# Narrower filler products at the start of a gated attention kernel, with a new order of its steps

## The chip, the cores and the metric

The kernel runs on one core of a Trainium2 chip. The metric is device time in microseconds (us); before the change it is 326.56 us, the median of three runs. One execution was also profiled, and all views of the profile in this document come from such an execution.

The core has five queues of instructions that run side by side, each in its own order: TensorE (PE; its weight loads stand apart as PEld), VectorE (DVE), ScalarE (ACT), GpSimd (POOL) and SyncE (SP). Here SP issues nearly all transfers; POOL issues some, and ACT a few at the start and the end.

## The reference

Attention without a softmax, an RMS norm, and a causal gated unit, all in float32. Batch is 8, there are 8 heads of 64, 576 tokens, and a model width of 512.

```python
kv = np.einsum('bhsd,bhse->bhde', k, v)
out = np.einsum('bhsd,bhde->bhse', q, kv)
rms = np.sqrt(np.mean(out * out, axis=-1, keepdims=True) + 1e-06)
x = out / rms * g_norm              # then (B,H,S,D) -> (B,S,H*D)
...
gate_pre[t] = sum over k of conv_w[k] * xp[t + k]   # 5 taps, causal
gate = 1.0 / (1.0 + np.exp(-gate_pre))
val = x @ w_val
return gate * val @ w_out
```

The three weights of the gated unit arrive as 64-bit floats, and the kernel turns them into float32 itself.

## The kernel before

The order of everything is written out by hand. A text, PLAN, lists 1152 steps such as `kv_product 1 0`; a loop at the end calls the function of each name with those numbers, and each function issues its instructions at once. So PLAN sets the order on every queue. What waits for what follows from the data: an instruction waits only where its operands, or a buffer that it overwrites, are not ready.

**The steps of one batch.** load_q_rows (batches 0 and 1) or load_q bring q, load_half brings one half of the heads of k or v. turn_q_rows turns q on TensorE by products with an identity matrix (L469, into five PSUM banks named qTps), and sort_q copies the result into qT on ACT (L476); from batch 2 on turn_q does this on DVE (L455, L458). kv_product is 36 products of 64x64 for one half of the heads (L435), and kv_copy moves the result to kvbd on ACT (L443). raw_product or raw_pair multiply qT by it (L490, L507). Then comes the norm: square on ACT (L525), sums on DVE (L533), powers on POOL (L539), and normalise on ACT, eight instructions of 64 columns (L551), or for batch 0 in one instruction on DVE (L555). turn_x and keep_x (TensorE L566, ACT L573), or turn_blocks and move_blocks (DVE L579, transfers issued by POOL L587), put x with channels on the partitions into xT; halo copies the edges on POOL.

gate_start, four gate_tap and gate_end make the gate on ACT and DVE. val_product (L616), or for batches 2 to 7 val_fast with its sums (L666), multiplies by w_val. gated joins gate and value on DVE; out_product (L697, L704), or fast_product with its sums (L763), multiplies by w_out. store writes rows out from SP's queue (L796), store_last for the last rows also from ACT's.

**Weights.** stage_weight loads a piece of a weight as 64-bit words (L334), and narrow_weight makes float32 of it in eight small steps, three on ACT and five on DVE. `cw` holds the taps and g_norm; turn_cw and keep_cw turn it.

**The opening.** q, k and v of batch 0 and two pieces of w_val are requested first. TensorE's first instructions are start_warm 36: products of an identity matrix whose result nothing reads. After them come turn_q_rows 0 0 to 0 4, kv_product 0 0 and 0 1, one keep_warm (another unread product, 512 columns wide, L426), turn_cw, and the first raw_product. The q of batch 1 is loaded into a buffer that turn_q_rows of batch 0 reads, and on SP's queue that load stands ahead of seven others: the rest of q, k and v of batch 1 and two pieces of w_val.

Of the kernel before, what the change touches and what calls it, by code (L numbers as in the profile page):

```python
# [21 lines left out]
turn_q_rows 0 1; sort_q 0 0; narrow_weight cw 0 0; turn_q_rows 0 2; sort_q 0 1; narrow_weight cw 0 1;  # L22
turn_q_rows 0 3; narrow_weight cw 0 2; sort_q 0 2; turn_q_rows 0 4; narrow_weight cw 0 3; sort_q 0 3;
kv_product 0 0; narrow_weight cw 0 4; load_q_rows 1 0; narrow_weight cw 0 5; sort_q 0 4; load_half k 1 0;
narrow_weight cw 0 6; narrow_weight cw 0 7; load_half v 1 0; load_q_rows 1 1; kv_product 0 1; load_half k 1 1;
stage_weight wval 2; keep_warm 1; turn_cw; stage_weight wval 3; kv_copy 0; load_half v 1 1; raw_product 0 3;
load_half k 2 0; narrow_weight wval 0 0; raw_product 0 2; keep_cw; square 0 3; narrow_weight wval 1 0;
raw_product 0 4; sums 0 3; load_half v 2 1; square 0 2; raw_product 0 1; narrow_weight wval 0 1; powers 0 3;
sums 0 2; raw_product 0 0; load_half v 2 0; square 0 1; square 0 4; narrow_weight wval 0 2; powers 0 2;
normalise 0 3; narrow_weight wval 1 1; sums 0 1; narrow_weight wval 1 2; turn_x 0 3; sums 0 4; keep_x 0 3;  # L30
powers 0 4; normalise 0 2; square 0 0; narrow_weight wval 0 3; sums 0 0; turn_x 0 2; powers 0 1;
narrow_weight wval 1 3; turn_q_rows 1 0; normalise 0 4; narrow_weight wval 0 4; keep_x 0 2; turn_q_rows 1 1;
narrow_weight wval 1 4; sort_q 1 0; narrow_weight wval 0 5; powers 0 0; turn_x 0 4; normalise 0 1; sort_q 1 1;
turn_q_rows 1 2; narrow_weight wval 1 5; keep_x 0 4; narrow_weight wval 0 6; turn_x 0 1; halo 0;
turn_q_rows 1 3; normalise 0 0; keep_x 0 1; narrow_weight wval 0 7; sort_q 1 2; turn_x 0 0;
narrow_weight wval 3 0; sort_q 1 3; kv_product 1 0; keep_x 0 0; gate_start 0 0; turn_q_rows 1 4;
gate_start 0 1; gate_tap 0 0 3; kv_product 1 1; load_q 2 0; narrow_weight wval 3 1; narrow_weight wval 1 6;
narrow_weight wval 3 2; val_product 0 0 1; gate_tap 0 0 2; kv_copy 1; narrow_weight wval 1 7; load_half k 2 1;
sort_q 1 4; stage_weight wout 0; narrow_weight wval 2 0; gate_start 0 2; gate_tap 0 1 3; raw_product 1 3;
narrow_weight wval 3 3; gate_tap 0 2 3; raw_product 1 2; square 1 3; gate_tap 0 1 2; narrow_weight wval 2 1;  # L40
val_product 0 1 1; sums 1 3; square 1 2; gate_tap 0 2 2; narrow_weight wval 2 2; powers 1 3; load_q 2 2;
narrow_weight wval 3 4; keep_val 0 0 1; raw_product 1 1; sums 1 2; keep_val 0 1 1; narrow_weight wval 2 3;
narrow_weight wval 3 5; powers 1 2; turn_q 2 0; raw_product 1 0; load_q 2 1; square 1 1; normalise 1 3;
val_product 0 0 0; sums 1 1; narrow_weight wval 2 4; stage_weight wout 2; powers 1 1; gate_tap 0 0 1;
square 1 0; normalise 1 2; raw_product 1 4; narrow_weight wval 3 6; turn_x 1 3; narrow_weight wval 2 5;
sums 1 0; val_product 0 1 0; square 1 4; narrow_weight wval 2 6; load_q 2 3; keep_x 1 3; powers 1 0;
gate_tap 0 1 1; normalise 1 1; narrow_weight wval 3 7; turn_x 1 2; kv_product 2 0; narrow_weight wout 0 0;
keep_x 1 2; sums 1 4; stage_weight wout 3; narrow_weight wval 2 7; narrow_weight wout 0 1; powers 1 4;
turn_x 1 1; gate_tap 0 0 0; narrow_weight wout 0 2; kv_product 2 1; gate_tap 0 2 1; narrow_weight wout 0 3;
turn_q 2 1; normalise 1 0; val_product 0 2 1; narrow_weight wout 0 4; load_q 3 0; turn_q 2 2; keep_x 1 1;  # L50
narrow_weight wout 2 0; keep_val 0 1 0; val_product 0 2 0; normalise 1 4; narrow_weight wout 0 5;
narrow_weight wout 0 6; keep_val 0 0 0; val_sums 0; kv_copy 2; stage_weight wout 1; gate_tap 0 1 0; turn_x 1 0;
load_q 3 1; narrow_weight wout 2 1; val_product 0 3 1; turn_q 2 3; keep_x 1 0; gate_end 0 0;
narrow_weight wout 2 2; gated 0 0; turn_x 1 4; narrow_weight wout 2 3; raw_pair 2 3; narrow_weight wout 0 7;
load_half k 3 0; keep_x 1 4; keep_val 0 2 0; narrow_weight wout 3 0; gate_tap 0 2 0; val_product 1 0 1;
square 2 3; load_q 3 2; square 2 2; sums 2 3; keep_val 0 2 1; gate_end 0 1; sums 2 2; powers 2 3;
val_product 1 0 0; gate_end 0 2; narrow_weight wout 2 4; gate_start 0 3; load_half v 3 0;
narrow_weight wout 2 5; gated 0 1; narrow_weight wout 3 1; powers 2 2; narrow_weight wout 2 6;
val_product 1 1 1; normalise 2 3; turn_q 3 0; narrow_weight wout 2 7; load_q 3 3; keep_val 1 0 0; halo 1;
turn_q 3 1; val_product 0 3 0; normalise 2 2; gate_tap 0 3 3; load_half v 3 1; narrow_weight wout 1 0;  # L60
keep_val 0 3 1; gate_tap 0 3 2; load_half k 3 1; raw_pair 2 1; keep_val 1 1 1; keep_val 1 0 1; turn_blocks 2 3;
narrow_weight wout 1 1; raw_product 2 4; turn_blocks 2 2; square 2 1; val_product 1 1 0;
narrow_weight wout 1 2; sums 2 1; square 2 0; gated 0 2; powers 2 1; keep_val 0 3 0; narrow_weight wout 3 2;
gate_tap 0 3 1; val_product 1 2 1; narrow_weight wout 1 3; load_q 4 0; sums 2 0; square 2 4;
narrow_weight wout 3 3; powers 2 0; sums 2 4; gate_tap 0 3 0; normalise 2 1; val_product 1 2 0;
narrow_weight wout 3 4; narrow_weight wout 1 4; powers 2 4; normalise 2 0; turn_blocks 2 1; val_product 1 3 1;
narrow_weight wout 1 5; narrow_weight wout 3 5; turn_q 3 2; normalise 2 4; narrow_weight wout 1 6; load_q 4 1;
kv_product 3 0; gate_end 0 3; narrow_weight wout 3 6; gate_start 1 0; gated 0 3; turn_x 2 4; val_product 1 3 0;
turn_blocks 2 0; keep_x 2 4; gate_start 1 2; narrow_weight wout 3 7; move_blocks 2 3; keep_val 1 1 0;
narrow_weight wout 1 7; gate_start 1 1; kv_product 3 1; gate_tap 1 0 3; keep_val 1 3 0; gate_tap 1 0 2;  # L70
out_product 0 1; kv_copy 3; load_half k 4 1; gate_tap 1 1 3; keep_val 1 2 0; turn_q 3 3; keep_val 1 2 1;
keep_val 1 3 1; gate_tap 1 0 1; load_q 4 2; gate_tap 1 0 0; move_blocks 2 2; gate_tap 1 2 3; raw_pair 3 3;
gate_tap 1 2 2; out_product 0 3; square 3 3; gate_tap 1 2 1; gate_end 1 0; sums 3 3; square 3 2; keep_out 0 1;
gated 1 0; powers 3 3; sums 3 2; store 0 1; gate_start 1 3; gate_tap 1 1 2; out_product 0 0; keep_out 0 3;
gate_tap 1 2 0; powers 3 2; load_half k 4 0; gate_tap 1 1 1; gate_end 1 2; store 0 3; gate_tap 1 3 3;
normalise 3 3; gate_tap 1 1 0; move_blocks 2 1; gate_tap 1 3 2; out_product 0 2; gate_end 1 1; load_half v 4 1;
gate_tap 1 3 1; keep_out 0 0; normalise 3 2; gate_tap 1 3 0; store 0 0; gated 1 1; gate_end 1 3; gated 1 2;
raw_pair 3 1; load_half v 4 0; gated 1 3; turn_q 4 0; raw_product 3 4; move_blocks 2 0; square 3 1;
out_product 0 4; turn_blocks 3 3; square 3 0; sums 3 1; load_q 4 3; val_sums 1; square 3 4; powers 3 1;
turn_q 4 1; turn_q 4 2; load_q 5 0; out_product 0 5; turn_blocks 3 2; keep_out 0 4; sums 3 0; normalise 3 1;  # L80
sums 3 4; powers 3 0; val_sums 2; turn_blocks 3 1; x_sums 2 2; out_product 0 7; halo 2; normalise 3 0;
val_sums 3; weight_sums 0; x_sums 2 0; gate_start 2 2; powers 3 4; keep_out 0 2; gate_tap 2 2 3;
gate_start 2 1; kv_product 4 0; x_sums 2 1; normalise 3 4; turn_q 4 3; kv_product 4 1; load_half v 5 0;
turn_blocks 3 0; load_q 5 1; gate_tap 2 2 2; turn_x 3 4; kv_copy 4; val_fast 2 0 0; x_sums 2 3; keep_x 3 4;
gate_start 2 0; gate_tap 2 1 3; raw_pair 4 3; store 0 4; move_blocks 3 3; val_keep 2 0 0; gate_tap 2 2 1;
val_fast 2 0 1; square 4 3; square 4 2; load_half v 5 1; sums 4 3; val_fast 2 0 2; gate_tap 2 2 0; powers 4 3;
val_fast 2 0 3; val_keep 2 0 2; sums 4 2; val_keep 2 0 1; keep_out 0 5; weight_sums 1; val_fast 2 0 4;
gate_end 2 2; store 0 5; powers 4 2; val_fast 2 0 5; val_keep 2 0 4; keep_out 0 7; gate_tap 2 0 3;
# [106 lines left out]
def kernel(  # L195
# [11 lines left out]
    nc = tc.nc  # L207
# [631 lines left out]
```

## Time and profile before

| | |
|---|---|
| three runs | 326.56, 325.11, 326.56 us |
| the profiled execution | 325.28 us |
| its span, first to last instruction | 323.5 us |
| mean granted TensorE clock | 0.994 |
| data moved by transfers | 55.50 MB, 172 GB/s on average |
| L697, 128 passes | 57.3 us busy |
| L421, 72 passes | 15.6 us busy |
| L435, the 1008 passes from buffers of k and v | 17.0 us busy |

A row of a group gives busy time, which can overlap itself on TensorE, since matmuls are pipelined. A product in float32 is two passes in the profile, so its count is twice that in the code. "Idle" is time of that engine alone.

### The profile page before, as it was taken

Reading aid. Unit: us, or ns where it says so; the run is one execution under the profiler, and the core shown is the slowest. Engines: PE = TensorE matmul, PEld = TensorE weight load, DVE = VectorE, ACT = ScalarE, POOL = GpSimd, SP = SyncE. Lnnn points to the kernel's source line nnn. Section 1 sums busy time; section 2 is a strip of 40 time slices with the busy share of each in tenths; the row PEclk is TensorE's granted clock in tenths of the full one; section 3 lists DMA queues with packets and bytes.
Section 4 is the critical chain, followed back from the end, with each engine's and each line's share of the span. In section 5 each row is a group of like instructions: output and inputs, shape, how many; then the busy total and the mean of one; then the engine's idle time right before and its main releaser. Section 6 shows DMA issues by size and latency. Waiting matters only on the chain.

```text
span 323.5 us, 8361 instructions
## 1 busy us (share of the span) xinstructions
PE 314.0 (97%) x3195; PEld 228.9 (71%) x3195; DVE 253.0 (78%) x451; ACT 191.7 (59%) x542; POOL 137.0 (42%) x177
## 2 busy tenths in 40 slices
PE   8998899999999999999999999999999999999994
PEld 8996787777754557566766667577758885888583
DVE  1014869999999997899899898999997989576612
ACT  1046689999959465785765868566863453224120
POOL 2003808334359447582866366578909200000000
PEclk9999799999999999999999999999999999999999
DMA  7819959699577929887976997322135303122233
GB/s 278 292 32 371 373 159 316 169 268 289 161 201 195 299 53 263 259 243 209 253 178 204 247 284 218 96 66 66 33 97 134 85 13 74 27 65 65 58 75 97
DMA packets 26696, 55.50 MB, mean 172 GB/s; under 512 B 6166, under 2 KB 8214, under 8 KB 26656
## 3 DMA queue, kind: packets, MB, share of 16 engines
q1 hardware_dynamic: 22608, 46.61, 49.8%
q0 software_dynamic: 3168, 6.32, 8.1%
q10 hardware_dynamic: 880, 2.03, 1.7%
q8 instruction: 25, 0.41, 0.6%
q14 instruction: 15, 0.12, 0.2%
HBM read 39.21 MB, written 9.44 MB: 150 GB/s over the span
## 4 chain that ended last, share of the span: by engine, by line
PE 85%; ACT 8%; DMA 3%; DVE 1%; POOL 1%; issue 1%; POOLq 0%; DVEq 0%; ACTq 0%
PE out L697 17%; PE va L666 14%; PE a L763 8%; PE vc L666 7%; PE cb L763 7%; PE val L616 6%; PE warm L421 5%; PE raw L435 5%; PE raw L507 3%; ACT x L551 3%; PE qTps L469 3%; PE out L704 3%; PE vb L666 3%; PE raw L490 2%; DMA v<-in_v_dram 2%; PE xTps L566 1%
## 5 line engine op out<-in xcount | busy, mean ns | idle before, releaser
L539 POOL TENSOR_TENSOR rt<-ss,mhalf 128x8 f32<-128x8 f32 (+1 forms) x40 | 71.7, 1805 | 85.1 <-DVE ss L533 85.0
L604 DVE SCALAR_TENSOR_TENSOR gate<-xT,cwT,gate 128x576 f32<-128x576 f32 x128 | 100.8, 809 | 5.2 <-ACT gate L598 4.7
L587 POOL DMA_DIRECT2D xT<-y x96 | 53.0, 558 | 28.9 <-ACT gv L675 8.2
L551 ACT ACTIVATE x<-raw,rt 128x64 f32<-128x64 f32 x252 | 55.9, 368 | 2.7 <-POOL rt L539 2.7
L697 PE MATMUL out<-wout,gv 128*128 128x512 f32 x128 | 57.3, 595 | 0.0
L697 PEld LDWEIGHTS out<-wout,gv 128*128 128x128 f32 x128 | 24.0, 190 | 26.1 <-issue 24.3
L616 PE MATMUL val<-xT,wval 128*128 128x288 f32 x128 | 33.0, 410 | 0.2 <-ACT xT L573 0.2
L525 ACT ACTIVATE sq<-raw 128x512 f32<-128x512 f32 (+1 forms) x40 | 21.6, 561 | 14.2 <-PE raw L507 10.1
L533 DVE TENSOR_REDUCE ss<-sq 128x8 f32<-128x520 f32 (+1 forms) x40 | 24.7, 632 | 6.4 <-ACT sq L525 6.2
L611 ACT ACTIVATE gate<-gate 128x576 f32<-128x576 f32 x32 | 22.1, 704 | 10.3 <-DVE gate L604 10.2
L616 PEld LDWEIGHTS val<-xT,wval 128*128 128x128 f32 x128 | 23.5, 190 | 6.5 <-ACT xT L573 0.3
L666 PE MATMUL va<-xs,vsum 128*128 128x288 f32 x96 | 27.2, 406 | 0.0
L629 DVE TENSOR_TENSOR gv<-gv,gate 128x576 f32<-128x576 f32 x32 | 23.6, 750 | 3.2 <-ACT gv L687 1.6
L598 ACT ACTIVATE gate<-xT,cwT 128x576 f32<-128x576 f32 x32 | 25.2, 796 | 0.9 <-DVE gv L629 0.9
L666 PEld LDWEIGHTS va<-xs,vsum 128*128 128x128 f32 x96 | 18.2, 190 | 4.9
L712 ACT COPY ot<-out 128x512 f32<-128x512 f32 x20 | 11.9, 594 | 15.7 <-PE out L704 8.7
L435 PEld LDWEIGHTS raw<-v,k 64*64 64x64 f32 x1008 | 15.6, 135 | 4.3 <-issue 1.7
L772 DVE TENSOR_TENSOR ot<-cb,ot 128x256 f32<-128x256 f32 x16 | 6.7, 420 | 13.9 <-ACT ot L776 7.9
L507 PEld LDWEIGHTS raw<-kvbd,qT 64*64 64x64 f32 x768 | 12.3, 134 | 7.1 <-issue 2.7
L435 PE MATMUL raw<-v,k 64*64 64x64 f32 x1008 | 17.0, 220 | 0.3 <-issue 0.3
L579 DVE STREAM_TRANSPOSE y<-x 128x512 f32<-128x512 f32 x24 | 16.5, 692 | 0.9 <-ACT x L551 0.9
L421 PE MATMUL warm<-ident 128*128 128x32 f32 x72 | 15.6, 401 | 1.4 <-POOL ident masks.py:199 1.4
(112 smaller groups left out, 523.3 us busy)
## 6 DMA issues: line engine op xcount, KB each, us to landing
qs<-in_q_dram SPq DMA_DIRECT2D x96, 140.0 KB, 4.8
out_dram<-ot SPq DMA_DIRECT2D x140, 64.0 KB, 1.8
k<-in_k_dram SPq DMA_DIRECT2D x14, 576.0 KB, 6.3
v<-in_v_dram SPq DMA_DIRECT2D x12, 576.0 KB, 6.7
xT<-y POOLq DMA_DIRECT2D x96, 64.0 KB, 3.6
y<-in_moe_w_val_dram SPq DMA_DIRECT2D x4, 512.0 KB, 11.1
w_wout<-in_moe_w_out_dram SPq DMA_DIRECT2D x4, 512.0 KB, 5.3
qs<-in_q_dram SPq DMA_DIRECT2D x3, 576.0 KB, 5.3
```

The source lines that it names most:

```text
L421: nc.tensor.matmul(warm_bank()[:, 0, 0:TB], ident[:], ident[:, 0:TB], start=True, stop=True)
L435: nc.tensor.matmul(raws[r * D:(r + 1) * D, s, i * D:(i + 1) * D], st["k", b, i][rows, r, cols], st["v", b, i][rows, r, cols], start=(j == ...
L533: nc.vector.reduce_sum(out=ss[:, 0:n], in_=st["sq", b, c][:, 0:n], axis=AX.X)
L539: nc.gpsimd.tensor_tensor(out=rt[:, 0:n], in0=st["ss", b, c][:, 0:n], in1=mhalf[:, 0:n], op=ALU.pow)
L551: nc.scalar.activation(out=x[:, to * D:(to + 1) * D], in_=one, func=AF.Copy, scale=st["rt", b, c][:, h:h + 1])
L587: nc.gpsimd.dma_start(out=xTs[b % 2][i * TB:(i + 1) * TB, :, first:first + P], in_=y[a * TB:(a + 1) * TB, i])
L598: nc.scalar.activation(out=gate[:], in_=xTs[b % 2][:, jt, HALO:SX], func=AF.Copy, scale=cwT[:, K - 1, jt:jt + 1])
L604: nc.vector.scalar_tensor_tensor(out=gate[:], in0=xTs[b % 2][:, jt, tap * TB:tap * TB + S], scalar=cwT[:, tap, jt:jt + 1], in1=gate[:], op ...
L616: nc.tensor.matmul(val[:], wval[:, kc, jt * P:(jt + 1) * P], xTs[b % 2][:, kc, HALO + n * SV:HALO + (n + 1) * SV], start=(kc == 0), stop=( ...
L666: nc.tensor.matmul(st[bank, "val", b, mj][:], weights_[:, k], tokens()[:, k], start=(n in (0, 1, 3) and k == 0), stop=(k == NK // 2 - 1), ...
L697: nc.tensor.matmul(po[:], gv[:, jt, first:first + P], wout[:, jt, :], start=(jt == 0), stop=(jt == NK - 1),)
L763: nc.tensor.matmul(st[bank, i, p], tokens()[:, k], weights_[:, k], start=(n < 2 and k == 0), stop=(k == NK // 2 - 1), skip_group_check=True)
```

## The change

Two things change. The filler product uses the first 32 columns of the identity as weights, where it used all 128, and writes 32 rows of its PSUM bank in place of 128. The count of 36 stays.

```diff
     def start_warm(n):
         for _ in range(n):
-            nc.tensor.matmul(warm_bank()[:, 0, 0:TB], ident[:], ident[:, 0:TB], start=True, stop=True)
+            nc.tensor.matmul(warm_bank()[0:TB, 0, 0:TB], ident[:, 0:TB], ident[:, 0:TB], start=True, stop=True)
```

And PLAN's steps stand in another order. The steps are the same but for one more `keep_warm 1`; most move by 10 to 20 places. The opening, cut to what TensorE and SP do:

```diff
 start_warm 36; turn_q_rows 0 0; turn_q_rows 0 1; sort_q 0 0; ... turn_q_rows 0 4;
-kv_product 0 0; load_q_rows 1 0; load_half k 1 0; load_half v 1 0; load_q_rows 1 1; kv_product 0 1; load_half k 1 1;
-stage_weight wval 2; keep_warm 1; turn_cw; stage_weight wval 3; kv_copy 0; load_half v 1 1; raw_product 0 3;
+kv_product 0 0; load_q_rows 1 0; load_half k 1 0; load_half v 1 0; load_q_rows 1 1; keep_warm 1; kv_product 0 1;
+load_half k 1 1; stage_weight wval 2; keep_warm 1; turn_cw; stage_weight wval 3; kv_copy 0; load_half v 1 1; raw_product 0 3;
 ...
-turn_x 0 3; turn_x 0 2; turn_q_rows 1 0; turn_q_rows 1 1; turn_x 0 4; turn_q_rows 1 2; turn_x 0 1; turn_q_rows 1 3;
-turn_x 0 0; kv_product 1 0; turn_q_rows 1 4; kv_product 1 1; val_product 0 0 1;
+turn_x 0 3; turn_x 0 2; kv_product 1 0; turn_x 0 4; turn_q_rows 1 0; turn_q_rows 1 1; turn_x 0 1; turn_q_rows 1 2;
+turn_x 0 0; turn_q_rows 1 3; turn_q_rows 1 4; kv_product 1 1; val_product 0 0 1;
```

Farther on, the loads of k and v change places too, as do the gates, sums and stores between them. From load_half v 4 1 to the kv_product that reads it there were 52 steps and are now 22; from load_half k 7 1 there were 71 and are now 24; from load_half k 6 1 there were 28 and are now 83.

## The prediction

> **What bounds the kernel now.** I read the page's busy row first, then the chain of work that ended last, then the opening in detail: the transfers' landings, the rows of one tile at a time, the waits of SP's queue, and busy time by stretch.
>
> ```profile
> PE 314.0 (97%) x3195; PEld 228.9 (71%) x3195; DVE 253.0 (78%) x451; ACT 191.7 (59%) x542; POOL 137.0 (42%) x177
> PE 85%; ACT 8%; DMA 3%; DVE 1%; POOL 1%; issue 1%; POOLq 0%; DVEq 0%; ACTq 0%
> ```
>
> TensorE is the bound: busy for 314.0 of 323.5 us and 85% of the chain. So a microsecond of TensorE that does no needed work is a microsecond of the end, as long as what follows can move up. The chain (start us, us, what) shows such work at its head:
>
> ```profile
> 1.36 15.57 PE warm L421 x72
> 16.93 5.31 PE qTps L469 x72
> 22.24 2.26 PE raw L435 x144
> 24.50 1.07 PE warm L426 x2
> 25.61 0.23 PE cwps L405
> 25.85 2.00 PE raw L490 x16
> ...
> 40.99 1.21 PE raw L435 x72
> 42.19 0.59 PE qTps L469 x8
> 42.78 1.21 PE raw L435 x72
> 43.99 2.14 PE val L616 x8
> ```
>
> The fillers, L421, hold TensorE from 1.36 to 16.93; 36 products are 72 passes (an f32 product stands as two), 15.57 / 72 = 216 ns each. Are they waiting room for data? The transfers issued in the first 4 us (last column: us from issue to landing):
>
> ```profile
> v<-in_v_dram ACTq DMA_DIRECT2D x2, 576.0 KB, 9.4
> k<-in_k_dram SPq DMA_DIRECT2D x2, 576.0 KB, 9.2
> y<-in_moe_w_val_dram SPq DMA_DIRECT2D x2, 512.0 KB, 11.8
> qs<-in_q_dram ACTq DMA_DIRECT2D x1, 576.0 KB, 5.5
> qs<-in_q_dram SPq DMA_DIRECT2D x1, 576.0 KB, 5.3
> ```
>
> Both parts of q are issued at 0.74 us, so they are in at 6.0 and 6.25. The two halves of k and v, issued from 1.20 to 1.70, land in pairs at about 9.4 and 12.4. All that turn_q_rows and kv_product need is there long before 16.93; only the fillers ahead of it in TensorE's queue hold it back. They hold the loads back too: SP's queue stands behind the release of the q buffer.
>
> ```profile
> SPq L319 <- PE qTps L469: 16.0, 1, 16.0
> ```
>
> **The clock in the opening.** The granted clock reads 1.00 there, but durations (min/median/max ns) say otherwise. First the fillers' rows, then L469 before and after 19.4 us:
>
> ```profile
> L421 PEld LDWEIGHTS warm<-ident x72: 287/333/333, 1.4 to 16.5; 128*128 128x128 f32 x72
> L421 PE MATMUL warm<-ident x72: 401/401/421, 1.4 to 16.5; 128*128 128x32 f32 x72
> ...
> L469 PEld LDWEIGHTS qTps<-ident,qs x24: 183/230/230, 16.9 to 19.1; 128*64 128x64 f32 x24
> L469 PE MATMUL qTps<-ident,qs x22: 421/421/477, 16.9 to 19.1; 128*64 128x128 f32 x22
> ...
> L469 PE MATMUL qTps<-ident,qs x50: 272/273/354, 19.3 to 22.0; 128*64 128x128 f32 x50
> L469 PEld LDWEIGHTS qTps<-ident,qs x46: 137/137/138, 19.5 to 21.9; 128*64 128x64 f32 x46
> ```
>
> The same product takes 421 ns before 19.4 and 273 after, and all fillers have the slow figures. So 15 us of fillers did not raise the clock; 2.5 us of real products did.
>
> **The change, part by part.**
>
> *1. Fillers.* Weights of 32 columns, 32 rows of output; the count stays 36. A slow load took 333 ns for 128 columns and 230 for 64: 103 ns per 64 columns, so 1.6 ns a column, 51 ns for 32. At 216 ns a pass the old filler is just the load of its 128 columns; the 32 moving columns (53 ns at the slow rate, from L469's pairs of 128 columns every 213 ns) lie under it. A new pass is then the larger of 51 and 53 ns. Here a rule speaks against: the Trainium skill, "TensorE: Matmul & The Clock Gate", Part 3, says that a load overlaps running matmuls only when its row group differs. These all use the same rows, so by the rule a pass is 51 + 53 = 104 ns and the 72 end at 1.36 + 7.5 = 8.9 us. But L490 has 128 columns of weights (a load row of 190 ns) and 128 moving on the same rows, and its 16 passes take 2.00 us, 125 ns each: loads do overlap. I take 60 ns, 72 x 60 = 4.3, end at 5.7 us, with ends at 53 ns (5.2 us) and 104 ns (8.9 us).
>
> *2. turn_q_rows of batch 0* now waits for q: start 6.3 us. Its 36 pairs cost 213 ns slow (7.7 us in all) or 109 fast (3.9). The same page, Part 1, has one busy window of about 3.4 us of any sustained activity raise the clock: by it the new fillers, or even the old, do so, and the turn costs 3.9. The trace speaks against counting on it (fillers slow to the end). I take one window slow: 16 pairs are 3.4 us, 20 fast are 2.2, end at 11.9 us. Both ends, 3.9 and 7.7, stay in the range.
>
> *3. kv_product 0 0* (1.13, half of the 2.26 row; its data in at 9.4): 13.0. *The added keep_warm* (a second L426 pair, 1.07): 14.1; it is on the path unless kv_product 0 1's data were late, which they are not (12.4). kv_product 0 1: 15.2; the old keep_warm: 16.3; turn_cw 0.25: 16.5. So raw_product 0 3 starts at about 16.5 in place of 25.85: **-9.3 us**. Fast from the first pair it is 14.9 (-11.0); slow through the whole turn 18.7 (-7.2). kv_copy (two of 0.37 on ACT) lies under the second keep_warm, as before. The narrow_weight cw steps are small (0.2 to 0.4 each) and now meet sort_q on ACT: three of 0.40 behind the first sort_q of 0.59 still end before 15.
>
> *4. SP's queue.* The 16.0 us wait ends at about 12 in place of 22.3, so eight loads (two q, four k and v, two wval, in both orders) go out some 10 us sooner. Before, they landed at 26.2 to 37.7, one each 1.5 us. The first wval pieces occupy the engines until about 15, so they now land at about 16.6 to 27. kv_product 1 1 needs the last of them; it ran at 42.78, and 10 us earlier is 32.8: covered by nearly 6 us. POOL has nothing but its three small loads and the identity before the first powers; nothing is pushed behind those.
>
> *5. The searched order*, everything up to the last val_product 0 step and beyond. No step is dropped or added but one keep_warm, so TensorE's needed work is the same. Two stretches have something to win or lose (columns: PE, PEld, DVE, ACT, POOL busy, granted clock, DMA share, GB/s):
>
> ```profile
> 30.00:34.50 4.50, 2.12 (x14) 1.40 (x12) 3.26 (x7) 4.43 (x9) 4.38 (x4) 0.84 1.06 373
> 34.50:36.50 2.00, 2.00 (x21) 2.00 (x22) 2.00 (x5) 0.74 (x3) 2.00 (x2) 0.50 1.07 385
> 50.00:60.00 10.00, 9.74 (x171) 7.79 (x173) 9.97 (x19) 9.95 (x35) 8.59 (x5) 1.00 0.94 274
> 60.00:80.00 20.00, 19.85 (x244) 15.44 (x235) 18.73 (x36) 19.68 (x58) 5.75 (x8) 1.00 0.86 237
> ```
>
> From 30 to 34.5 TensorE idles 2.4 us for the first x of batch 0, and the clock then drops to half, about 1.7 us more. kv_product 1 0 now stands inside that gap, so up to 2 us can be won; if its data come late it stays a gap. From 50 to 80 TensorE, DVE and ACT are all nearly full; DVE and ACT start 10 us earlier as well, since their first work hangs on the products of step 3, so the stretch moves as a whole. Steps move by some 10 to 20 places either way there and after; I count them at 0 with 1.5 us to either side. Their cover is that TensorE has little idle time to lose or win after 80 us; where the cover is gone, a late DVE or ACT step costs its own 0.4 to 0.8 us each time.
>
> **Sum.** -9.3 against the profiled execution's own 325.28 us (span 323.5) gives 316.0. The median shown, 326.56, is 1.3 above that and the lowest, 325.11, 0.2 below; I add 0.7: **316.7 us**. The case's own range: 325.28 + 0.7 less 7.2 - 1.5 is 320.3, and 325.28 less 11.0 + 2 is 312.3; 312 to 320.
>
> **The rivals.**
>
> *Half the gain is given back (about 321.4).* From 49 to 68 us the chain runs through ACT's normalise (L551) and wexp steps: DVE 9.97 and ACT 9.95 of 10. If narrowing the weights, which must wait for wval's last pieces (now about 24 and 25.5 us), bunches against the earlier normalise, TensorE waits there and 9.3 / 2 is kept. For it: two full engines. Against: both idle for most of the first 20 us, and in the new order too their work begins with the products.
>
> *The fillers do not shrink (about 326).* If the pass of 216 ns is not the weight columns but a cost per product, the opening stays as it was and only the order and one keep_warm (+1.1) are left: within 1.5 us of before. Against it: L435 and L507, 64 columns, pass every 16 to 17 ns four abreast, so no such floor exists.
>
> *Slower: a load that SP issues too late (about 330).* SP's queue is in order, and stores that wait for their ot tile stand ahead of loads (the row below). The new order puts load_half v 4 1 only 22 steps ahead of its kv_product, behind store 0 3 (52 steps before), and load_half k 7 1 24 steps (71 before). 1152 steps in 323.5 us are 0.28 us each: 22 steps are 6.2 us, and such loads take 6.7 us (v) and 6.3 (k) to land. At its plan place the cost is 0.5 us; if the store ahead stalls by more than that, each microsecond is one of TensorE's, and a q or k load queued behind it is late too. Both loads fully exposed are 13.0, net of 9.3 it is +3.7. It decides from 9.3 us of such waits on. Against: SP runs ahead of the plan whenever its waits allow, and a load that is 28 steps ahead (k 6 1) did no visible harm.
>
> ```profile
> SPq L796 <- DVE ot L772: 53.2, 8, 10.6
> ```
>
> **How the numbers follow.** What a measurement can tell from no change is about 0.5%, 1.6 us. The full gain 0.75; half given back 0.11; fillers unchanged 0.05, of it most within 0.5%; late loads 0.09. Faster 0.87, same 0.04, slower 0.09. The range, 312.0 to 321.5, is the likeliest case's with the middle of the second; what is left out is the last two cases and the tail of the second.
>
> **What would show it.** Right: L421's 72 passes end near 5.7 us with load rows well under 333 ns; the first L469 at about 6.3; L490 first at 15 to 18.7; SP's wait on qTps about 6 us in place of 16.0; val_product near 34; TensorE busy about 304. Wrong: L421 passes still 200 ns apart; a gap of TensorE before L435 of batch 4 or 7 released by a DMA; or the time of val_product moved by 9 us and the end by less, with TensorE waits on DVE or ACT between 35 and 70 us.

## The result, and the profile after

The changed kernel takes 316.4 us (median of four runs, 315.48 to 316.86) against 326.4 for the kernel before: ratio 0.970, 95% interval 0.967 to 0.973. The forecast was 316.7, in a range of 312.0 to 321.5. The profiled execution took 316.86 us, its span 315.1.

First the busy row and the engines' shares of the chain that ended last, then that chain's opening (start us, us, what), of the kernel after.

```profile
PE 301.9 (96%) x3197; PEld 215.6 (68%) x3197; DVE 254.5 (81%) x451; ACT 191.6 (61%) x542; POOL 138.0 (44%) x177
PE 88%; ACT 5%; DMA 4%; issue 1%; DVE 1%; ACTq 0%; DVEq 0%
```

```profile
1.68 12.43 DMA v<-in_v_dram
14.15 1.28 PE raw L435 x72
15.43 1.07 PE warm L426 x2
16.54 0.23 PE cwps L405
16.78 2.00 PE raw L490 x16
...
26.14 2.03 PE raw L435 x72
...
34.10 1.21 PE raw L435 x72
35.31 2.14 PE val L616 x8
```

TensorE is still the bound, 12 us less busy. The fillers are gone from the head of the chain; what stands there now is the landing of the second half of v. raw_product 0 3 (the first L490 row) starts at 16.78 in place of 25.85 (-9.1 us), the first val_product (L616) at 35.31 in place of 43.99 (-8.7), and the span is 8.4 shorter. So the gain is made in the opening, and 0.7 us of it is lost on the way.

The rows of one tile each, for the fillers and the first turn of q, and the transfers issued in the first 4 us with their time to landing:

```profile
L421 PEld LDWEIGHTS warm<-ident x72: 113/157/157, 1.4 to 4.7; 128*32 128x32 f32 x72
L421 PE MATMUL warm<-ident x72: 196/241/263, 1.4 to 4.7; 128*32 128x32 f32 x72
...
L469 PEld LDWEIGHTS qTps<-ident,qs x72: 132/137/137, 6.3 to 10.1; 128*64 128x64 f32 x72
L469 PE MATMUL qTps<-ident,qs x72: 272/273/323, 6.3 to 10.2; 128*64 128x128 f32 x72
```

```profile
v<-in_v_dram ACTq DMA_DIRECT2D x2, 576.0 KB, 10.4
k<-in_k_dram SPq DMA_DIRECT2D x2, 576.0 KB, 10.2
y<-in_moe_w_val_dram SPq DMA_DIRECT2D x2, 512.0 KB, 13.5
```

The 72 filler passes fit between 1.4 and 4.9 us. Inside them, at 4.04 us, their duration changes from 241 to 196 ns and the time from one start to the next from 53 to 32: the clock has risen. The turn of q therefore has no slow product (273 ns is the median, where the slow ones took 421). The loads tell the other half: k and v took 9.2 and 9.4 us before, in the mean of their two halves, and 10.2 and 10.4 now. The first half lands at 9.4 to 9.5, nearly as before; the second at 13.9 (k) and 14.1 (v), 1.7 us late. TensorE is ready at 12.7 and waits 1.4 us.

SP's queue was released early, as its waits show:

```profile
SPq L319 <- PE qTps L469: 4.2, 1, 4.2
```

And one loss that before had too, 8.5 us later (columns: PE, PEld, DVE, ACT, POOL busy, granted clock, DMA share, GB/s):

```profile
22.00:26.00 4.00, 1.63 (x8) 1.13 (x8) 3.99 (x8) 2.88 (x5) 4.00 (x3) 0.81 1.09 364
26.00:30.00 4.00, 4.00 (x103) 3.69 (x104) 4.00 (x9) 1.37 (x3) 3.10 (x6) 0.76 1.05 389
```

TensorE waits twice for the first x of batch 0 (1.76 and 1.28 us), and the clock is at half from 24.5 to 27.9 us; kv_product 1 0 (L435 at 26.14) takes 2.03 us in place of 1.21.

### The profile page after: what moved, and what is told of

It reads as the page before. It is cut to its first block, busy times and chain, and to the rows that moved or that the text cites. A ratio compares the mean times of both kernels' runs of the same rounds, so it can differ in the third digit from the quotient of the medians.

```text
span 315.1 us, 8369 instructions
## 1 busy us (share of the span) xinstructions
PE 301.9 (96%) x3197; PEld 215.6 (68%) x3197; DVE 254.5 (81%) x451; ACT 191.6 (61%) x542; POOL 138.0 (44%) x177
## 3 DMA queue, kind: packets, MB, share of 16 engines
q10 hardware_dynamic: 880, 2.03, 1.9%
## 4 chain that ended last, share of the span: by engine, by line
PE 88%; ACT 5%; DMA 4%; issue 1%; DVE 1%; ACTq 0%; DVEq 0%
PE out L697 18%; PE va L666 15%; PE val L616 8%; PE a L763 8%; PE vc L666 8%; PE cb L763 7%; PE raw L435 6%; PE out L704 5%; PE raw L507 4%; DMA v<-in_v_dram 4%; PE vb L666 4%; PE raw L490 3%; PE xTps L566 2%; ACT sq L525 1%; PE qTps L469 1%; ACT x L551 1%
## 5 line engine op out<-in xcount | busy, mean ns | idle before, releaser
L539 POOL TENSOR_TENSOR rt<-ss,mhalf 128x8 f32<-128x8 f32 (+1 forms) x40 | 69.7, 1749 | 86.8 <-DVE ss L533 83.8
L587 POOL DMA_DIRECT2D xT<-y x96 | 52.9, 557 | 16.2 <-issue 5.3
L533 DVE TENSOR_REDUCE ss<-sq 128x8 f32<-128x520 f32 (+1 forms) x40 | 24.9, 628 | 10.6 <-ACT sq L525 9.5
L616 PE MATMUL val<-xT,wval 128*128 128x288 f32 x128 | 33.0, 409 | 0.0
L616 PEld LDWEIGHTS val<-xT,wval 128*128 128x128 f32 x128 | 23.6, 190 | 6.0 <-issue 0.2
L435 PEld LDWEIGHTS raw<-v,k 64*64 64x64 f32 x1008 | 15.6, 135 | 6.9 <-issue 3.5
L435 PE MATMUL raw<-v,k 64*64 64x64 f32 x1008 | 16.8, 220 | 2.2 <-DMA v<-in_v_dram 1.4
L579 DVE STREAM_TRANSPOSE y<-x 128x512 f32<-128x512 f32 x24 | 16.5, 693 | 0.8 <-ACT x L551 0.8
L507 PEld LDWEIGHTS raw<-kvbd,qT 64*64 64x64 f32 x768 | 12.3, 134 | 7.0 <-issue 3.9
L455 DVE STREAM_TRANSPOSE qT<-qs 128x512 f32<-128x512 f32 x24 | 16.6, 690 | 0.0
## 6 DMA issues: line engine op xcount, KB each, us to landing
y<-in_moe_w_val_dram SPq DMA_DIRECT2D x4, 512.0 KB, 12.5
```

The lines of the kernel that those rows point to most:

```text
L435: nc.tensor.matmul(raws[r * D:(r + 1) * D, s, i * D:(i + 1) * D], st["k", b, i][rows, r, cols], st["v", b, i][rows, r, cols], start=(j == ...
L507: nc.tensor.matmul(st["raw", b, x][cols, r, hp * D:(hp + 1) * D], st["qT", b][rows, hp, x * P + half * D:x * P + (half + 1) * D], kv_bd[b ...
L539: nc.gpsimd.tensor_tensor(out=rt[:, 0:n], in0=st["ss", b, c][:, 0:n], in1=mhalf[:, 0:n], op=ALU.pow)
L587: nc.gpsimd.dma_start(out=xTs[b % 2][i * TB:(i + 1) * TB, :, first:first + P], in_=y[a * TB:(a + 1) * TB, i])
L616: nc.tensor.matmul(val[:], wval[:, kc, jt * P:(jt + 1) * P], xTs[b % 2][:, kc, HALO + n * SV:HALO + (n + 1) * SV], start=(kc == 0), stop=( ...
```

## Experiments

A comparison gives the ratio to the kernel before, run in turn with it on the same chip. The times of "first raw_product" and of landings are from each kernel's own profiled execution.

### One part at a time: fillers without the order, order without the fillers

filler_only has the PLAN of before and the new filler line alone; order_only has the new PLAN with the old filler line.

> The order of before, with the 32-column fillers alone. My theory: the gain is the fillers' time (-9.1 us at the first raw_product) and the order only carries it through, so this kernel takes about 317.5 us (316 to 319.5), raw_product 0 3 starts at about 16.8 and the fillers end at 4.7. Rival, the order earns a real part: 320 us or more, with the early start lost again between raw_product 0 and the first val_product. Rival, the order costs: under 315.5 us.

> The new order with the fillers of 128 columns as before. My theory: one more keep_warm of 1.07 us on the path and an order that neither gains nor loses: 327.5 us (326 to 329), fillers to 16.9 and raw_product 0 3 at about 27. Rival, the order earns by itself: under 325 us. Rival, the order fits only the early start: over 330 us.

filler_only took 316.71 us (ratio 0.970, 0.964 to 0.975), the same median as both parts together; its first raw_product started at 17.16. order_only took 326.74 against 325.42 (ratio 1.004, 1.001 to 1.007), with the first raw_product at 27.16, 1.3 us later than before, of which the second keep_warm is 1.07. So the fillers alone bring the gain, and the searched order as a whole adds nothing that these runs can tell.

Within filler_only there is more to see. Its four executions took 316.50, 316.92 and 317.02 us at a mean granted clock of 0.989, and 313.70, less than any of the changed kernel, at 0.997. The profiled one is of the slower three: TensorE waits for k, and the clock is at half from 15.19 to 18.60, so that the keep_warm behind the wait takes 1.87 us in place of 1.12.

```profile
13.66 1.35 PE L435 MATMUL raw<-v,k 64*64 64x64 f32 x72 [2.15 <-DMA k<-in_k_dram]
14.94 1.87 PE L426 MATMUL warm<-kvbd,ident 128*128 128x512 f32 x2
```

In the changed kernel the added keep_warm stands in that wait, and its profile shows no half clock there. So the new order may win by its keep_warm and lose as much elsewhere. No run has the old order with the keep_warm alone.

### Short, wide fillers, and none

Both have the new PLAN. short_wide has 9 fillers with the old filler line of 128 columns; no_filler has no start_warm step.

```diff
-start_warm 36;
+start_warm 9;
```

> The new order with 9 fillers of 128 columns, so that they end at about 5.2 us like the 36 narrow ones but, as in before, do not raise the clock. Theory that time is what counts: turn_q_rows runs 421 ns products for 3.4 to 6.8 us and ends at 11.5 to 13.5, the late half of k and v covers most of it, and the kernel takes 317 us (316 to 318.5). Rival, that the narrow fillers are worth it by the clock that they raise: 319.5 us or more, with raw_product 0 3 after 19 us.

> The new order with no filler product at all; turn_q_rows 0 0 is TensorE's first work, at 6.3 us. Theory that time is what counts: as with short fillers, a slow start of 3.4 to 6.8 us inside turn_q_rows, largely covered by the landing of the second half of k and v: 317 us (316 to 318.5). Rival, that the clock decides: 319.5 us or more.

no_filler took 316.4 us (ratio 0.972, 0.966 to 0.978), the changed kernel's median. But its four executions lie in two pairs: 314.70 and 314.98 us at a mean granted clock of 1.000, 317.83 and 318.41 at 0.987 and 0.988. The profiled execution is of the slower pair. Its chain shows a slow turn of q and no wait for k and v:

```profile
6.06 6.67 PE qTps L469 x72
12.73 1.21 PE raw L435 x72
13.94 1.06 PE warm L426 x2
14.99 1.21 PE raw L435 x72
```

The turn takes 6.67 us, 2.5 more than in the changed kernel (4.15), yet the first raw_product starts at 17.55, only 0.8 later, because there TensorE had to wait for v anyway. The time that the old fillers took is what cost 9 us; that the narrow ones are needed to win it back, no run shows.

short_wide took 319.44 us (ratio 0.983, 0.979 to 0.986), the rival's number, but not for the rival's reason: its clock was up from 8.65 us and its turn of q was done at 11.38. What it has that no_filler has not is a hole of 2.17 us inside kv_product 0 1, in which TensorE waits for no other instruction:

```profile
16.89 0.46 PE L435 MATMUL raw<-v,k 64*64 64x64 f32 x14 [2.17 <-issue]
```

The hole and, from 18.89 to 22.30, a half clock put the first val_product at 38.97, 3.7 us later than in the changed kernel. The next kernel separates the clock in the turn from the hole.

### Wide weights that are used densely

```diff
-nc.tensor.matmul(warm_bank()[:, 0, 0:TB], ident[:], ident[:, 0:TB], start=True, stop=True)
+nc.tensor.matmul(warm_bank()[:, 0, :], ident[:], ident[:], start=True, stop=True)
```

This is the filler line of short_wide (9 of them) with 128 moving columns in place of 32.

> The changed kernel with 9 fillers of 128 columns of weights and 128 moving columns, in place of 36 of 32 and 32; it differs from short_wide only in the moving columns. Theory that the clock rises by the share of time in which columns move, whatever the weights: the clock rises inside the fillers or within the first 2 us of turn_q_rows, which then runs 273 ns products, and the kernel takes 316.5 us (315.5 to 318). Rival, that the loads of wide weights keep the clock down: 421 ns products from 6.3 us on, as in short_wide, and 319.4 us.

Rows of the two tiles, and TensorE's timeline with the hole (in brackets: idle before, and what ended it):

```profile
L421 PEld LDWEIGHTS warm<-ident x18: 285/333/333, 1.4 to 4.9; 128*128 128x128 f32 x18
...
L469 PE MATMUL qTps<-ident,qs x72: 272/273/323, 6.2 to 10.1; 128*64 128x128 f32 x72
```

```profile
12.55 1.14 PE L435 MATMUL raw<-v,k 64*64 64x64 f32 x58
15.91 0.46 PE L435 MATMUL raw<-v,k 64*64 64x64 f32 x14 [2.22 <-issue]
```

The clock rose at 6.03 us, so that the whole turn of q ran at 273 ns: the theory of moving columns holds in this execution, and wide weights as such do not keep the clock down. Yet the kernel took 319.47 us (ratio 0.980, 0.976 to 0.983), the rival's number once more, with the same hole in the same place: after 58 passes of kv_product 0 1. Behind it the clock is at half from 16.27 to 23.09. My expectation of the time was wrong in both kernels.

### What holds up the second half of k and v

My first theory was the loads of batch 1, which now go out at 10.5 us. late_loads puts them behind kv_product 0 1, by a product that reads q's buffer:

```diff
-load_q_rows 1 0; ... load_half k 1 0; ... load_half v 1 0; load_q_rows 1 1; keep_warm 1; kv_product 0 1;
+... keep_warm 1; kv_product 0 1; hold_q; load_q_rows 1 0; load_half k 1 0; load_half v 1 0; load_q_rows 1 1;
+    def hold_q():
+        nc.tensor.matmul(warm_bank()[0:TB, 0, 0:TB], ident[:, 0:TB], qs[:, 0, 0, 0:TB], start=True, stop=True)
```

> The changed kernel, with one narrow filler product that reads q's buffer after kv_product 0 1, and the loads of batch 1 behind it on SP's queue, so that the first of them goes out at about 14 us in place of 10.5. Theory that these loads, started early, hold up the second half of k and v and both pieces of wval (14.1, 15.4 and 16.9 us in the changed kernel against 12.4, 13.7 and 15.1 before): they land at the old times again, kv_product 0 1 starts at 12.7 in place of 14.15, raw_product 0 3 at about 15.4, and the kernel takes 315.2 us (314 to 315.9). Rival, that this wait is given back by the later loads or by ACT's chain before turn_x: 316 us or more.

```profile
13.90 1.54 PE L438 MATMUL raw<-v,k 64*64 64x64 f32 x72 [1.28 <-DMA k<-in_k_dram]
```

The first load of batch 1 went out at 15.65, and k still landed at 13.77 and v at 13.55. The time was 317.05 us (ratio 0.972, 0.970 to 0.975). The theory is refuted: those loads had not begun when k and v were late.

What had begun is another kind of transfer. The page lists it under the queues, here of the kernel after:

```profile
q8 instruction: 25, 0.41, 0.6%
```

25 packets of 16 KB. TensorE has 3197 matmuls and as many weight loads, 6394 instructions: 256 for each packet, which is 64 bytes each. no_filler has 144 instructions fewer and 24 packets, gap_fill (below) 160 more and 26. So this queue seems to bring TensorE's own instructions. The holes confirm it. Counted in TensorE's matmuls and weight loads, the holes of short_wide and dense_wide stand behind the same number, 449; other holes inside kv_product, in these and other kernels, stand behind 961, 1217, 1474, 1730, 2242 and 3777, each a multiple of 256 from 449, to within one. And each ends 1.2 to 1.5 us after the end of one of these packets. In such a hole TensorE waits for its instructions.

The packets' records in the trace give the time of the first one inside the program, about 1.1 us long. (The landings are those of the half that came first and of the other.)

| kernel | first packet starts, us | second half of k and v lands | second wval piece lands | hole in kv_product 0 1 |
|---|---|---|---|---|
| before | 18.3 | 12.2, 12.4 | 15.1 | none |
| after | 10.2 | 13.9, 14.1 | 16.9 | none |
| filler_only | 9.9 | 13.3, 13.5 | 16.3 | none |
| late_loads | 9.8 | 13.6, 13.8 | 16.3 | none |
| dense_wide | 13.5 | 12.1, 12.4 | 16.2 | 2.22 |
| short_wide | 14.3 | 12.2, 12.4 | 16.7 | 2.17 |
| no_filler | 14.3 | 12.3, 12.5 | 15.2 | none |

Where the packet starts at about 10 us, k and v are late; where it starts at 13.5 or later, they are not, but in two of four cases TensorE runs out of instructions before it has come. The other profiled executions agree: in the five with narrow fillers the packet starts at 9.6 to 10.2 us and the second half lands at 13.3 to 13.7, and order_only is like before. half_count tries this with the width of the weights and the fillers' length unchanged (the counts are those of start_warm):

```diff
-nc.tensor.matmul(warm_bank()[0:TB, 0, 0:TB], ident[:, 0:TB], ident[:, 0:TB], start=True, stop=True)       # 36
+nc.tensor.matmul(warm_bank()[0:TB, 0, 0:2 * TB], ident[:, 0:TB], ident[:, 0:2 * TB], start=True, stop=True)   # 18
```

> The changed kernel with 18 fillers of 64 moving columns in place of 36 of 32: the same weights and the same 3.8 us, but 72 TensorE instructions fewer. Theory that a 16 KB load of TensorE's own instructions, which starts at 10.2 us in the changed kernel (at 13.5 and 14.3 with 9 wide fillers or none), is what holds up the data of that time by 1.1 to 1.4 us: it moves to 11 to 13.5 us, the second half of k and v lands at 12.1 to 12.9 in place of 13.3 to 14.1, and TensorE stands inside kv_product 0 1 for its instructions, 1 to 2 us; time 316.5 to 318.5. Rival, that the load of batch 1's q holds the data up: they land at 13.3 or later, and the time is 316.4.

```profile
12.74 0.81 PE L435 MATMUL raw<-v,k 64*64 64x64 f32 x40 [0.19 <-DMA k<-in_k_dram]
14.12 0.69 PE L435 MATMUL raw<-v,k 64*64 64x64 f32 x32 [0.57 <-issue]
```

The packet moved to 11.7 us, the second half landed at 12.4 and 12.6 although the load of batch 1's q had gone out at 10.31, as in filler_only (10.32), and TensorE had a hole of 0.57 us behind its 449th instruction, smaller than I expected. The time, 315.95 us (ratio 0.970, 0.967 to 0.972), was below my range: the wait and the hole, 0.76 us together, are less than the changed kernel's wait of 1.4. This edit shows that the delay goes with the packet. How the packet delays the data is not shown; that the two share a transfer engine is an explanation that fits the landings of k and v in every row. In no_filler a packet of 14.3 us left the wval piece on time, so not every transfer is hit. The packet alone was not taken away.

### The gaps before turn_x

```diff
-raw_product 0 0; ... turn_x 0 3; sums 0 1; ... turn_x 0 2;
+raw_product 0 0; fill_gap 24; ... turn_x 0 3; fill_gap 16; sums 0 1; ... turn_x 0 2;
+    def fill_gap(n):
+        ...
+        for _ in range(n):
+            nc.tensor.matmul(st["gap"][0:TB, 0:TB], ident[:, 0:TB], ident[:, 0:TB], start=True, stop=True)
```

> The changed kernel with 24 narrow filler products behind raw_product 0 0 and 16 between turn_x 0 3 and turn_x 0 2, where TensorE waits 1.8 and 1.3 us. Theory that these gaps bring on the half clock of 24.5 to 27.9 us, which costs up to 1.7 us: no granted clock under 1 from 20 to 30 us in the profile, 315.5 us (314.5 to 316.2). Rival, that the half clock is hidden under ACT's chain there: the clock stays up, and the time stays at 316.4.

> Both edits together: later loads of batch 1, and the gaps filled. If both theories hold the gains add up: 314.2 us (313 to 315.2). If the start of ACT's chain is what counts and not TensorE's clock: as late_loads alone.

TensorE's timeline in gap_fill:

```profile
20.73 1.71 PE L407 MATMUL gap<-ident 128*32 128x32 f32 x48
22.56 0.66 PE L572 MATMUL xTps<-ident,x 128*128 128x128 f32 x4
23.14 1.20 PE L407 MATMUL gap<-ident 128*32 128x32 f32 x32
24.49 0.66 PE L572 MATMUL xTps<-ident,x 128*128 128x128 f32 x4 [0.15 <-ACT xT L579]
```

gap_fill took 315.08 us (ratio 0.967, 0.965 to 0.969). The clock stayed full from 6.6 us to the end, and the first val_product stood at 33.86, 1.45 earlier than in the changed kernel. late_and_gap took 315.17 (ratio 0.968, 0.965 to 0.971): the later loads add nothing, as they did alone. A second comparison put gap_fill and the changed kernel beside each other, which the first had not:

> The changed kernel once more, on the same chip as the next three, for comparison: 316.4 us (315.4 to 317), and a half clock between about 20 and 30 us in the profile.

> The changed kernel with narrow fillers in the two gaps before turn_x, once more. If the gain of the first comparison is real, 315.1 us (314.6 to 315.7) and 1.0 to 1.5 us below after_again; rival, it was the chip and the phase of the clock's windows: within 0.5 us of after_again.

after_again took 316.02 us (315.11 to 316.87; ratio 0.970, 0.967 to 0.973) and gap_fill_again 315.15 (314.90 to 315.61; ratio 0.967, 0.965 to 0.970). gap_fill has the lower median both times, by 1.3 us against the changed kernel's first runs and by 0.9 side by side, and the lowest of all versions; its interval overlaps the changed kernel's, so a gain of about 1 us is likely and not certain. Nor is it shown to be the clock's: the changed kernel's executions at a granted clock of 1.000 took 315.11 to 316.50 us. The profile of after_again missed my expectation: there the clock rose only at 10.43 us, after the fillers and most of the turn, and did not fall at all later.

```profile
6.11 6.24 PE qTps L469 x72
...
17.17 2.00 PE raw L490 x16
```

It is the same program. What differs is shown by the records of the granted clock. It changes only in steps: the stretches between two changes last 3.41, 6.83, 10.24, 13.65 us and so on, multiples of 3.41. This grid lies differently in each execution. In the profile of the changed kernel 2.5 us of the two waits before turn_x fall into one step, and the clock is at half behind it; in after_again the border between two steps parts them into 1.76 and 1.28 us, in order_only into 1.55 and 1.49, and it stays up.

### The old order with all of this

old_order_filled is filler_only with a keep_warm ahead of kv_product 0 1 and the same two filled gaps (their bank is the one that turn_q_rows 1 0 takes next).

> The order of before with the narrow fillers, a keep_warm ahead of kv_product 0 1, and the two gaps before turn_x filled as in gap_fill. Theory: the old order's chain from raw_product to the second turn_x is some 2 us shorter than the new one's (5.9 us against 8.2), and with the clock kept up that is gained at the first val_product (33.5 us): 314.5 us (313.3 to 315.5). Rival, the new order earns as much after that: 315.5 to 316.5.

It took 319.81 us (ratio 0.979, 0.975 to 0.984), a clear miss: five executions took 318.96 to 320.79 us at a granted clock of 0.989 to 0.993, the sixth 316.06 at 0.999. Up to the first val_product the profiled one (320.68) did as gap_fill (33.95 and 33.86). Then TensorE's timeline and the stretches show why (columns as above):

```profile
53.02 0.90 PE L441 MATMUL raw<-v,k 64*64 64x64 f32 x18 [2.76 <-issue]
```

```profile
50.00:54.00 4.00, 1.24 (x37) 0.98 (x26) 3.97 (x10) 4.00 (x16) 0.01 (x1) 0.82 0.43 129
54.00:60.00 6.00, 6.00 (x14) 4.32 (x15) 2.12 (x5) 1.52 (x4) 0.00 (x0) 0.55 0.83 252
```

A hole of 2.76 us, inside kv_product of batch 2 and behind TensorE's 1730th instruction, for which the packet of queue 8 starts only at 50.5; then 6.8 us at half clock. In gap_fill the hole behind the same count is 0.60 us, as its packet starts at 47.75. The extra filler instructions put the border of a packet there; why it comes later in the old order is not shown. Whether the old order could do without the hole is open: no run has it with filled gaps and another count.

## Why the prediction was right, point by point

Forecast and median agree to 0.3 us, which is in part luck: the executions of either kernel differ by about 1.4 us, and the profiled ones moved by 8.4 us where the forecast had 9.3. What was right is the mechanism, that the fillers' time goes and the end follows; two terms inside the sum were wrong.

*Step 1, the fillers.* Right: 53 ns a pass at the slow clock, the lower end of the two bounds, so loads do overlap on the same rows, and the rule of the Trainium skill ("TensorE: Matmul & The Clock Gate", Part 3), that they overlap only on other rows, does not hold here. The fillers were over at 4.9 us, not 5.7, as the clock rose inside them.

*Step 2, the turn of q.* The start, 6.3, was right. One window of slow products was wrong: the turn took 4.1 us, ending at 10.4 and not 11.9. The term's failing was to take "fillers do not raise the clock" over from the old ones. By the forecast's own rates the old pass moved columns for 53 of 213 ns and the new one all the time; dense_wide shows that this share counts. On Part 1 of the same page, by which one busy window of 3.4 us raises the clock, the traces agree in part: in the changed kernel it rose 2.7 us after the first filler, but 15.6 us of the old ones did not raise it, so what merely occupies TensorE is not all busy. It is also not sure: after_again had a slow turn all the same.

*Step 3, kv_product.* Wrong in a way that nearly cancelled the error of step 2. I had the second half of k and v in at 12.4 and the added keep_warm on the path. They landed at 14.1, and keep_warm (11.6 to 12.7) lay in that wait and cost nothing. Forecast for the first raw_product 16.5, measured 16.78: -9.1 in place of -9.3, with 1.5 us won in the turn, 1.5 lost by the late data, and 0.3 in the lengths of the pieces. That the two errors cancel is luck. The sum does not hang on it: in after_again the turn was slow as forecast (to 12.35), keep_warm was on the path, no data were waited for, and raw_product stood at 17.17; no_filler (17.55) and filler_only (17.16) are not far off either.

*Step 4, SP's queue.* The wait on qTps ended at 10.5, not 12; the loads landed at 18.3 to 28.8 us, not 16.6 to 27, as the wval pieces ahead of them were late too (16.9 in place of 15.1). kv_product 1 1 needed the last one at 34.1: covered, as forecast.

*Step 5, the order at nothing.* Right for the whole: order_only is 1.3 us over before, most of it the keep_warm of 1.07. That no part of the order wins or loses is not shown (see filler_only). The steps move less than was said: half of them by five places or fewer, a quarter by 12 or more. The 2 us that could be won in the gap before turn_x were not; the idle time moved, and the half clock stayed. From the first val_product to the end the time was the same within 0.3 us.

*The rivals.* Half given back: DVE and ACT were full between 46 and 56 us (9.97 of 10 each) and the start still came through. Fillers that do not shrink: refuted by the rows. Loads that SP issues too late: the products of batches 4 and 7 (L435 at 109 and 194 us) run without a wait. The one load of k or v that TensorE waited for was batch 0's, issued in the first 2 us.

## What to carry to other kernels

Look at the head of the chain for work that nothing reads, and compare its end with the landing of the data behind it: here 10.6 us of fillers stood after q had come. Try the kernel without fillers too: here it had the same median. A filler raised the clock by columns that move, not by weights that load, so make its weights as narrow as its moving side, and don't count on one to do so in each execution. Expect a start that is pulled forward to meet the transfers that used to have that time to themselves, TensorE's own instructions among them.

## What the runs showed of the hardware that was not expected

- TensorE's instructions come in packets of 16 KB, 256 instructions, that take about 1.1 us each. In the opening, one that started at about 10 us went with k and v 1.1 to 1.7 us late. Where one came after TensorE needed it, TensorE stood still for up to 2.76 us, always behind a fixed count of its instructions, and went on 1.2 to 1.5 us after the packet's end. The profile shows this as idle time ended by "issue" in the middle of a group.
- 15.6 us of products with 128-column loads and 32 moving columns left the clock low. With 32 and 32 it rose at 4.0 to 6.6 us in seven of eight profiled executions (10.4 in the eighth), and with 128 and 128 at 6.0.
- The granted clock changed only on a grid of 3.41 us, which lies differently in each execution. While it was full, it fell to half, for 3.41 or 6.83 us, at the end of steps in which TensorE was idle for 1.8 to 2.6 us (ten of eleven falls; the other, in short_wide, had 1.5), and in no other step before 300 us was TensorE idle for more than 1.76. So the same gap can cost a slow stretch in one execution and nothing in the next: no_filler took about 315 us at a mean granted clock of 1.000 and 318 at 0.987.
